# Strassen's algorithm inside the block products of the second feed-forward matmul, on one NeuronCore

## The chip, the cores and the metric

The kernel runs on one core of a Trainium2 chip. The metric is the device time of one execution in microseconds (us); less is better. Each time below is the median of several executions. "Before" is the kernel as it was and "after" the kernel with the change; PE is TensorE's matmul engine.

## The reference

The program is talking-heads attention, a Fourier mix, a normalization and a feed-forward network with a residual, all in float32. The change touches the second matrix product of the last line but one:

```python
u = x + np.real(fft2(x))                     # x: attention output, 8 x 448 rows of 768
un = (u - mean(u)) / sqrt(var(u) + 1e-6)
ch = np.maximum(un @ w_ch1, 0.0) @ w_ch2     # w_ch1: 768 x 3072, w_ch2: 3072 x 768
return u + ch
```

The 3584 rows are worked through in seven tiles of 512.

## The kernel before

Both feed-forward products already use Strassen's algorithm once, in the form with seven block products. For the second product the blocks of w2 (`w2f`) and their sums and differences (`w2s`) lie ready in DRAM; the sums were formed during the first tile. A tile of the second product is seven block products in the order `ORDER`, each of two halves of the contraction and two row blocks. The results that share a PSUM bank (keys P, Q and R) accumulate, and VectorE adds each of them into the residual `u`:

```python
def load_w2(i, half):
    w = pw2.tile([P, NQ, DH], F32, name="w2t", tag="w2t")      # 4 buffers
    of, n = {0: (w2f, 0), 1: (w2f, 2), ..., 6: (w2s, 0)}[i]    # cut
    nc.sync.dma_start(out=w[:, :, :], in_=of[n, half])
    return w

for n, i in enumerate(ORDER):                                  # 7 block products
    key = {0: "P", 5: "P", 6: "P", 3: "P", 1: "Q"}.get(i, "R")
    for half in range(2):
        w = load_w2(i, half)
        for x in range(NT2 // 2):                              # 2 row blocks
            ...
            for kf in range(NQ):                               # 6 steps
                nc.tensor.matmul(p, lhs[i][...], w[:, kf, :], ...)   # 384 columns
            if half == 0:
                continue
            for r, c in {...}[i]:                              # 1 or 2 quarters
                nc.vector.tensor_tensor(us_, us_, p, op=ALU.add)
    # after products 0 and 1: VectorE forms three differences of h each;
    # n = 1..4: normalization of the next tile
```

PE runs each float32 matmul of the code as two instructions. The framework, not the source, sets the order in which each engine gets its instructions. Each engine then works through its own queue in that order, as the traces show.

## Time and profile before

| | before |
|---|---|
| median, lowest and highest of 3 executions | 2750.27 us, 2742.7 to 2753.29 |
| attention and Fourier stage | to about 1113 us |
| preparation of the feed-forward | to 1155 us |
| second product, one tile | 111.0 us (the last 108.3) |
| second product, all seven tiles | 774.3 us |
| busy in the whole span: PE, VectorE (DVE), GpSimd (POOL) | 90%, 46%, 27% |
| mean granted clock of PE | 0.967 |

The lines that carry this are in the prediction. In short: in the second product PE is busy all the time and everything else has room, so this stage costs what the stream of matmuls costs.

### The profile page before, as it was taken

What the parts mean: (1) busy time and instruction counts of PE and PEld (TensorE: products, weight loads), DVE (VectorE), ACT (ScalarE), POOL (GpSimd) and SP (SyncE); (2) the same over time, 40 slices, a digit from 0 to 9 for tenths busy, and PEclk for the clock granted to TensorE, in tenths of its full rate; (3) what the DMA queues carried; (4) which work ended last, traced back from release to release, by engine and by line L of the source; (5) the groups of instructions that cost most, each with busy time, mean ns of one, the idle gap of its engine ahead of it and who ended that gap; (6) DMA issues with size and microseconds to landing.
All of it is one profiled execution on the core that took longest, in us unless ns stands there. A gap on an engine that the chain in (4) does not pass through costs nothing.

```text
span 2744.6 us, 46540 instructions
## 1 busy us (share of the span) xinstructions
PE 2476.4 (90%) x18544; PEld 1587.2 (58%) x18544; DVE 1262.2 (46%) x2238; ACT 724.0 (26%) x2135; POOL 732.0 (27%) x1117
## 2 busy tenths in 40 slices
PE   4778888888888886499999999999999999999998
PEld 2334344444444443387577678668658767866865
DVE  3887888888887876543032122213203212221220
ACT  2555555555555552110011001001001100100100
POOL 5465767666665544200100010010010000001000
PEclk7999999999999998799999999999999999999999
DMA  6665657575656457744444444444445444444432
GB/s 168 181 183 173 189 168 202 164 202 164 193 175 186 152 157 252 280 161 175 141 172 165 155 155 161 161 166 161 150 155 171 157 150 167 149 163 160 144 109 107
DMA packets 184471, 462.60 MB, mean 169 GB/s; under 512 B 23111, under 2 KB 129095, under 8 KB 171712
## 3 DMA queue, kind: packets, MB, share of 16 engines
q1 hardware_dynamic: 159968, 361.30, 38.7%
q0 software_dynamic: 24288, 98.33, 13.0%
q8 instruction: 148, 2.42, 0.4%
q14 instruction: 67, 0.55, 0.1%
HBM read 317.17 MB, written 59.79 MB: 137 GB/s over the span
## 4 chain that ended last, share of the span: by engine, by line
PE 41%; issue 9%; DMA 7%; DVE 1%; POOL 0%; SPq 0%; POOLq 0%; ACT 0%
PE psP L829 12%; PE psP L789 10%; PE psR L829 7%; PE psR L789 6%; PE psQ L829 3%; DMA w1t<-w1f 3%; PE psQ L789 2%; DMA u<-u_scr 2%; DMA out_dram<-u 2%; DMA w1t<-w1s 1%; PE psQ L759 1%; DVE st L746 0%; POOL ub L766 0%; DVE u L838 0%; SPq L703 0%
## 5 line engine op out<-in xcount | busy, mean ns | idle before, releaser
L789 PE MATMUL psP<-ub,w1t 128*128 128x256 f32 x2016 | 469.3, 386 | 26.6 <-DVE mv L748 16.9
L789 PEld LDWEIGHTS psP<-ub,w1t 128*128 128x128 f32 x2016 | 385.9, 193 | 94.7 <-DMA w1t<-w1f 22.1
L829 PE MATMUL psP<-w2t,h 128*128 128x384 f32 x1344 | 436.9, 486 | 0.0
L829 PEld LDWEIGHTS psP<-w2t,h 128*128 128x128 f32 x1344 | 254.4, 190 | 173.4
L323 ACT ACTIVATE PP<-mx,nmx 128x448 f32<-128x448 f32 x384 | 239.9, 629 | 376.2 <-DVE nmx L314 372.2
L766 POOL TENSOR_TENSOR ub<-ub 128x768 f32<-128x768 f32 x28 | 50.0, 1806 | 1036.2 <-ACT ub L761 1035.6
L336 POOL TENSOR_SCALAR PP<-PP,rcp 128x448 f32<-128x448 f32 x384 | 259.6, 686 | 154.0 <-DVE rcp L333 109.4
L307 PE MATMUL mx<-Kr,kw 60*64 60x448 f32 x1536 | 204.0, 589 | 97.0 <-ACT PP L323 88.2
L357 DVE STREAM_TRANSPOSE Pv<-po 128x896 f32<-128x896 f32 x192 | 212.9, 1109 | 101.4 <-PE po L346 101.2
L789 PE MATMUL psR<-ub,w1t 128*128 128x256 f32 x1008 | 232.1, 379 | 0.5 <-DMA w1t<-w1s 0.5
L314 DVE TENSOR_REDUCE nmx<-mx 128x2 f32<-128x896 f32 x192 | 206.2, 1074 | 34.9 <-PE mx L307 23.9
L829 PE MATMUL psR<-w2t,h 128*128 128x384 f32 x672 | 220.0, 486 | 0.0
L281 PE MATMUL ms<-kT,qT 64*64 64x448 f32 (+1 forms) x1536 | 205.3, 568 | 7.0 <-DVE X L475 6.3
L374 PEld LDWEIGHTS ms<-Pv,vv 64*64 64x64 f32 x5376 | 169.4, 142 | 67.2 <-issue 38.7
L128 ACT COPY Sb<-ms 124x448 f32<-124x448 f32 x379 | 186.5, 538 | 81.1 <-PE ms L281 66.1
L789 PEld LDWEIGHTS psR<-ub,w1t 128*128 128x128 f32 x1008 | 191.2, 190 | 27.8 <-DMA w1t<-w1s 1.9
L346 PE MATMUL po<-PP,kw 60*32 60x448 f32 x3072 | 194.1, 562 | 9.1 <-DVE rcp L333 7.7
L374 PE MATMUL ms<-Pv,vv 64*64 64x120 f32 x5376 | 181.0, 278 | 16.9 <-ACT Sb L128 15.4
L838 DVE TENSOR_TENSOR u<-u,psP 128x384 f32<-128x384 f32 x56 | 31.0, 554 | 341.6 <-PE psP L829 341.6
L829 PEld LDWEIGHTS psR<-w2t,h 128*128 128x128 f32 x672 | 126.3, 190 | 84.3
L307 PEld LDWEIGHTS mx<-Kr,kw 60*64 60x64 f32 x1536 | 42.2, 135 | 207.1 <-ACT PP L323 153.9
L761 ACT COPY ub<-psQ 128x384 f32<-128x384 f32 x56 | 25.0, 481 | 508.3 <-PE psQ L759 508.3
(92 smaller groups left out, 2604.4 us busy)
## 6 DMA issues: line engine op xcount, KB each, us to landing
Kr<-Sb SPq DMA_DIRECT2D x768, 105.0 KB
w2t<-w2s SPq DMA_DIRECT2D x56, 1152.0 KB
w2t<-w2f SPq DMA_DIRECT2D x42, 1152.0 KB
w1t<-w1s SPq DMA_DIRECT2D x72, 576.0 KB
raw<-in_moe_w_ch_dram POOLq DMA_DIRECT2D x96, 384.0 KB, 4.4
w1t<-w1f SPq DMA_DIRECT2D x84, 384.0 KB
w1t<-w1f SPq DMA_DIRECT2D x96, 192.0 KB
w1t<-w1s SPq DMA_DIRECT2D x72, 192.0 KB
```

What stands on the lines that cost most here:

```text
L128: self.nc.scalar.copy(out=out, in_=in_)
L281: nc.tensor.matmul(pss[x][64 * y:64 * y + r0 + 64 - lo, :S], st["qT", xx][64 * x:64 * x + 64, y, lo:r0 + 64], st["kT", xx][64 * x:64 * x + ...
L307: nc.tensor.matmul(mx[64 * z:64 * z + 64, x, :S], kw1[64 * x:64 * x + KR, :], Kr[64 * x:64 * x + KR, z, :], start=True, stop=True)
L314: nc.vector.tensor_reduce(nmx[:, :], steps[T]["mx"][:, :, :S], axis=AX.X, op=ALU.max, negate=True)
L323: nc.scalar.activation(PP[:, x, :], steps[T]["mx"][:, x, :S], ACTF.Exp, bias=steps[T]["nmx"][:, x:x + 1], accum_out=den[:, x:x + 1])
L336: nc.gpsimd.tensor_scalar(PP[:, x, :], PP[:, x, :], rcp[:, x:x + 1], 1.0, op0=ALU.mult, op1=ALU.mult)
L346: nc.tensor.matmul(po[o:o + 32, z, :S], kw2[64 * z:64 * z + KR, y, :], PP[64 * z:64 * z + KR, :, c * HS:(c + 1) * HS], start=True, stop=True)
L357: nc.vector.transpose(g["Pv"][:, T % GT, :].rearrange("p (z s) -> p z s", z=2), steps[T]["po"][:, :, :S])
L374: nc.tensor.matmul(pss[y][64 * x:64 * x + 64, :nu * R], st["v"][64 * y:64 * y + 64, i, jb * D:(jb + 1) * D], _ap(Pv, 64 * y * rp + 32 * jb ...
L766: nc.gpsimd.tensor_tensor(ub[:, o], ub[:, a], ub[:, b], op=ALU.subtract)
L789: nc.tensor.matmul(p, w[m][:, i, kc, :], ub[:, i, kc, :], start=opens and kc == 0, stop=kc == NK - 1, skip_group_check=True)
L829: nc.tensor.matmul(p, lhs[i][:, half * NQ + kf, x * P:(x + 1) * P], w[:, kf, :], start=opens and half == 0 and kf == 0, stop=half == 1 and ...
```

## The change

Strassen's algorithm is applied a second time, inside each of the seven block products. An outer product becomes seven inner products with half the rows, half the columns and half the contraction: 7 x 7 x 6 matmuls of 192 columns in place of 7 x 4 x 6 of 384, seven eighths of the columns. In exchange, every outer product needs four sums of w2's parts and four of h's parts, and more additions into `u`. The sums of w2 are formed while they are used, three on GpSimd and one on VectorE, one outer product ahead.

```diff
-    pw2 = pool("pw2", 4)
+    pw2 = pool("pw2", 9)
+    pss = pool("pss", 6)
     ...
+    def load_w2(i):
+        ... four parts b11, b12, b22, b21 are loaded
+        t1, t2, t4 = (w2_tile() for _ in range(3))
+        for o, x, y in ((t1, b12, b11), (t2, b22, t1), (b12, b22, b12), (t4, b21, t2)):
+            eng = nc.vector if o is b12 else nc.gpsimd
+            eng.tensor_tensor(o[:, :, :], x[:, :, :], y[:, :, :], op=ALU.subtract)
+        return b11, b21, b22, t4, t1, t2, b12
+
+    def sums_h(lhs):
+        ... s1, s2, s4, s3 = four tiles
+        for o, x, op, y in ((s1, a21, ALU.add, a22), (s2, s1, ALU.subtract, a11),
+                            (s4, a12, ALU.subtract, s2), (s3, a11, ALU.subtract, a21)):
+            nc.vector.tensor_tensor(o, x, y, op=op)
+        return a11, a12, s4, a22, s1, s2, s3
     ...
         for n, i in enumerate(ORDER):
-            ... two halves, two row blocks, 384 columns
+            bs, as_ = ready
+            for m, j in enumerate(INNER):             # INNER = 0, 1, 5, 4, 6, 2, 3
+                key = {0: "P", 5: "P", 6: "P", 3: "P", 1: "Q"}.get(j, "R")
+                ...
+                for kf in range(NQ):
+                    nc.tensor.matmul(p, as_[j][:, kf, :], bs[j][:, kf, :], ...)
+                for (r0, r1), (c0, c1) in PART[i]:    # result j into 1 to 4 parts of u
+                    nc.vector.tensor_tensor(us_, us_, ..., op=ALU.add)
+                if m == 1 and n + 1 < len(ORDER):
+                    ready = load_w2(ORDER[n + 1]), sums_h(lhs[ORDER[n + 1]])
```

The layouts of `w2f` and `w2s` in DRAM change to match (rows of 192 columns), and so does the code that forms w2's sums in the first tile; the pool of the normalized rows (`pun`) goes from two buffers to one. VectorE's sum, from here on "the own sum", is written over `b12`, which GpSimd's first sum reads. So the own sum must wait for GpSimd's first one.

More of the change, by code (lines that the diff above doesn't have):

```diff
@@ L634 @@
 ORDER = (0, 1, 4, 5, 2, 6, 3)
+INNER = (0, 1, 5, 4, 6, 2, 3)
+PART = {0: [((0, 2), (0, 2))], 1: [((0, 1), (0, 1))], 2: [((0, 1), (1, 2))],
+        3: [((1, 2), (0, 1))], 4: [((0, 2), (1, 2))],
+        5: [((0, 1), (1, 2)), ((1, 2), (0, 2))], 6: [((1, 2), (0, 2))]}
 NM = DFF // 2 // P
@@ L637 @@
 NQ = NM // 2
+DQ = DH // 2
 def _pieces(w_ch1, w_ch2, w1f, w2f):
@@ L655, in _pieces @@
             for j in range(2):
-                dst = w2f[2 * i + j, kf // NQ, :, kf % NQ, :]
+                dst = w2f[2 * i + j, kf // NQ, :, :, kf % NQ, :]
                 out.append((w_ch2, i * (DFF // 2) + kf * P, j * DH,
-                            dst.rearrange("p (m f) -> p m f", m=1), 1))
+                            dst.rearrange("m p f -> p m f"), 2))
     return out
@@ L671, in ffn_phase @@
     pw1 = pool("pw1", 3)
-    pw2 = pool("pw2", 4)
+    pw2 = pool("pw2", 9)
+    pss = pool("pss", 6)
     pu = pool("pu", 2)
-    pun = pool("pun", 2)
+    pun = pool("pun")
     pub = pool("pub")
@@ L714, in load_w1, with w2_tile @@
         return w
+    def w2_tile():
+        return pw2.tile([P, NQ, DQ], F32, name="w2t", tag="w2t")
     def sum_w2(kf):
-        w = pw2.tile([P, NQ, DH], F32, name="w2t", tag="w2t")
-        at = kf // NQ, slice(None), kf % NQ
-        nc.sync.dma_start(
-            out=w[:, 0:4, :],
-            in_=w2f[:, at[0], :, at[2], :].rearrange("b p d -> p b d"))
-        for o, a, b in ((4, 1, 0), (5, 3, 4), (1, 3, 1), (2, 2, 5)):
-            nc.vector.tensor_tensor(w[:, o], w[:, a], w[:, b], op=ALU.subtract)
@@ L724, in sum_w2 @@
-        for o, n in ((1, 0), (4, 2)):
-            nc.sync.dma_start(
-                out=w2s[n:n + 2, at[0], :, at[2], :].rearrange("b p d -> p b d"),
-                in_=w[:, o:o + 2, :])
-    def load_w2(i, half):
-        w = pw2.tile([P, NQ, DH], F32, name="w2t", tag="w2t")
+        at = kf // NQ, kf % NQ
+        ws = [w2_tile() for _ in range(4)]
+        b = []
+        for n in range(4):
+            t = ws[n // 2][:, 2 * (n % 2):2 * (n % 2) + 2, :]
+            nc.sync.dma_start(
+                out=t, in_=w2f[n, at[0], :, :, at[1], :].rearrange("c p d -> p c d"))
+            b.append(t)
@@ new lines, in sum_w2 @@
+        b11, b12, b21, b22 = b
+        t3, t1 = (ws[2 + n // 2][:, 2 * (n % 2):2 * (n % 2) + 2, :] for n in range(2))
+        t2, t4 = (ws[3][:, 2 * n:2 * n + 2, :] for n in range(2))
+        for o, x, y in ((t1, b12, b11), (t2, b22, t1), (t3, b22, b12), (t4, b21, t2)):
+            nc.vector.tensor_tensor(o, x, y, op=ALU.subtract)
+        for o, n in ((t3, 0), (t4, 1), (t1, 2), (t2, 3)):
+            nc.sync.dma_start(
+                out=w2s[n, at[0], :, :, at[1], :].rearrange("c p d -> p c d"), in_=o)
@@ L731, in load_w2 @@
+    def load_w2(i):
         of, n = {0: (w2f, 0), 1: (w2f, 2), 2: (w2f, 3), 3: (w2s, 1), 4: (w2s, 2),
                  5: (w2s, 3), 6: (w2s, 0)}[i]
-        nc.sync.dma_start(out=w[:, :, :], in_=of[n, half])
-        return w
+        w = {}
+        for r, c in ((0, 0), (0, 1), (1, 1), (1, 0)):
+            w[r, c] = w2_tile()
+            nc.sync.dma_start(out=w[r, c][:, :, :], in_=of[n, r, c])
+        b11, b12, b21, b22 = w[0, 0], w[0, 1], w[1, 0], w[1, 1]
+        t1, t2, t4 = (w2_tile() for _ in range(3))
[3 more added lines that the diff above has]
+        return b11, b21, b22, t4, t1, t2, b12
@@ new lines, in sums_h, with part @@
+    def sums_h(lhs):
+        def part(r, c):
+            return lhs[:, c * NQ:(c + 1) * NQ, r * P:(r + 1) * P]
+        a11, a12, a21, a22 = part(0, 0), part(0, 1), part(1, 0), part(1, 1)
+        s1, s2, s4, s3 = (pss.tile([P, NQ, P], F32, name="s", tag="s")[:, :, :]
+                          for _ in range(4))
+        for o, x, op, y in ((s1, a21, ALU.add, a22), (s2, s1, ALU.subtract, a11),
+                            (s4, a12, ALU.subtract, s2), (s3, a11, ALU.subtract, a21)):
+            nc.vector.tensor_tensor(o, x, y, op=op)
+        return a11, a12, s4, a22, s1, s2, s3
@@ L817, in second @@
         u = us.pop(t)
-        ps = {}
+        ru = _row(u)
+        ready = load_w2(ORDER[0]), sums_h(lhs[ORDER[0]])
         for n, i in enumerate(ORDER):
-            key = {0: "P", 5: "P", 6: "P", 3: "P", 1: "Q"}.get(i, "R")
-            opens = i in (0, 1, 4)
-            for half in range(2):
-                w = load_w2(i, half)
-                for x in range(NT2 // 2):
-                    if opens and half == 0:
-                        ps[key, x] = ps_tile(key)
-                    p = ps[key, x][:, :DH]
-                    for kf in range(NQ):
-                        nc.tensor.matmul(
-                            p, lhs[i][:, half * NQ + kf, x * P:(x + 1) * P], w[:, kf, :],
-                            start=opens and half == 0 and kf == 0,
-                            stop=half == 1 and kf == NQ - 1, skip_group_check=True)
-                    if half == 0:
-                        continue
-                    for r, c in {0: [(0, 0)], 1: [(0, 0)], 4: [(1, 1)], 5: [(0, 1)],
-                                 2: [(0, 1)], 6: [(1, 1)], 3: [(1, 0)]}[i]:
-                        us_ = u[:, 2 * r + x, c * DH:(c + 1) * DH]
-                        nc.vector.tensor_tensor(us_, us_, p, op=ALU.add)
@@ new lines, in second @@
+            bs, as_ = ready
+            ps = {}
+            for m, j in enumerate(INNER):
+                key = {0: "P", 5: "P", 6: "P", 3: "P", 1: "Q"}.get(j, "R")
+                if j in (0, 1, 4):
+                    ps[key] = ps_tile(key)
+                p = ps[key][:, :DQ]
+                for kf in range(NQ):
+                    nc.tensor.matmul(p, as_[j][:, kf, :], bs[j][:, kf, :],
+                                     start=j in (0, 1, 4) and kf == 0,
+                                     stop=kf == NQ - 1, skip_group_check=True)
+                r2, c2 = {0: (0, 0), 1: (0, 0), 4: (1, 1), 5: (0, 1), 2: (0, 1),
+                          6: (1, 1), 3: (1, 0)}[j]
+                for (r0, r1), (c0, c1) in PART[i]:
+                    dims = [[ru, P], [2 * DM, r1 - r0], [DH, c1 - c0], [1, DQ]]
+                    us_ = _ap(u, (2 * r0 + r2) * DM + c0 * DH + c2 * DQ, dims)
+                    nc.vector.tensor_tensor(
+                        us_, us_, _ap(ps[key], 0, [[_row(ps[key]), P], [0, r1 - r0],
+                                                   [0, c1 - c0], [1, DQ]]), op=ALU.add)
+                if m == 1 and n + 1 < len(ORDER):
+                    ready = load_w2(ORDER[n + 1]), sums_h(lhs[ORDER[n + 1]])
@@ L883 @@
     w1f = scr.tile([NM, P, 4, NK, P], F32, name="w1f")
-    w2f = scr.tile([4, 2, P, NQ, DH], F32, name="w2f")
+    w2f = scr.tile([4, 2, 2, P, NQ, DH // 2], F32, name="w2f")
     w1s = scr.tile([NM, P, 4, NK, P], F32, name="w1s")
-    w2s = scr.tile([4, 2, P, NQ, DH], F32, name="w2s")
+    w2s = scr.tile([4, 2, 2, P, NQ, DH // 2], F32, name="w2s")
     mix_phase(tc, ident, q, k, v, w_pre, w_post, u_scr,
```

## The prediction

> **What bounds the kernel now.** I read the page first: its busy table, its slices, its chain of waits and its groups; then the stretches by stage, then the timeline of single stretches. The kernel has three parts: an attention and Fourier stage to about 1113 us, a preparation to 1155 us, and seven tiles of the feed-forward from there to 2745 us.
>
> ```profile
> PE 2476.4 (90%) x18544; PEld 1587.2 (58%) x18544; DVE 1262.2 (46%) x2238; ACT 724.0 (26%) x2135; POOL 732.0 (27%) x1117
> ...
> PE   4778888888888886499999999999999999999998
> ...
> DVE  3887888888887876543032122213203212221220
> ...
> POOL 5465767666665544200100010010010000001000
> PEclk7999999999999998799999999999999999999999
> ```
>
> From slice 17 on, PE is at 9 with nothing near it: VectorE is at 0 to 3 tenths, GpSimd at 0 to 1, the clock is full. The second product (line 829) is part of that. Two tiles by stage, first product, then second (start:end, length, busy time of each engine with its instruction count):
>
> ```profile
> 1387.00:1505.00 118.00, 113.88 (x499) 95.03 (x498) 36.54 (x82) 16.50 (x44) 3.15 (x5) 0.99 0.48 160
> 1505.00:1616.00 111.00, 111.00 (x379) 69.52 (x378) 16.23 (x24) 5.77 (x14) 8.68 (x6) 1.00 0.43 157
> ```
>
> In the second product PE is busy 111.00 of 111.00 us, VectorE 16 us, GpSimd 9 us. So that stage is the matmul stream itself, and anything that shortens the stream shortens the kernel, as long as the other engines still fit beside it.
>
> How long is one instruction of that stream? The duration of a matmul includes its latency, so I take the spacing from the timeline:
>
> ```profile
> 1509.18 15.64 PE L829 MATMUL psQ<-w2t,h 128*128 128x384 f32 x48
> ...
> 1524.66 0.49 PE L759 MATMUL psQ<-ident,un 128*128 128x128 f32 x3
> ```
>
> The groups give 486 ns for one of line 829, so 48 of them in 15.64 us are spaced (15.64 - 0.486) / 47 = 322.4 ns. Line 789 has 256 columns, and the chain of waits shows 12 of them as pieces of 2.59 us, or 215.8 ns. The slope is (322.4 - 215.8) / 128 = 0.833 ns a column, with 2.5 ns fixed. A float32 product is two such instructions (1344 + 672 + 336 = 2352 at line 829 for the 1176 calls that the code makes).
>
> **What the Trainium skill says.** "TensorE: Matmul & The Clock Gate", section "LDWEIGHTS (loading the stationary operand)", makes a weight load columns / 1.2 ns, 107 ns for 128 columns. The trace shows 190 ns for each, which would exceed the new matmuls; but that includes a tail. Four loads of 113 columns, each about 178 ns long by the trace, occupy 0.49 us together, and their matmuls were 107 ns apart:
>
> ```profile
> 1089.58 0.49 PEld L416 LDWEIGHTS ms<-ident,XT 128*113 128x113 f32 x4 [0.35 <-ACT XT L396]
> ```
>
> So a load occupies the path for about 107 ns, and 192 columns (162 ns) hide it. "SBUF — State Buffer", section "Who interferes with whom", says that VectorE instructions with two SBUF inputs and GpSimd instructions that read SBUF exclude each other for a whole instruction. The trace agrees:
>
> ```profile
> 275.71 1.91 POOL L432 TENSOR_TENSOR xd<-X 112x768 f32<-112x768 f32 x1
> ...
> 275.98 2.05 DVE L521 SCALAR_TENSOR_TENSOR tmp<-raw,tmp 128x384 f32<-128x384 uint32 x1
> ```
>
> The VectorE instruction takes 0.514 us at its shortest. Here it began inside the GpSimd one (275.71 to 277.62) and ended at 278.03, 0.41 us after it. This lock is what my prediction turns on. "GPSIMD Engine Reference", section "Engine selection", advises against two-input elementwise work there, about 2 times slower; this trace has 1.80 us for 768 elements, where VectorE's line would give 0.96.
>
> **The change, part by part, for one tile.**
> *Matmuls.* Before: 336 instructions x 322.4 = 108.3 us. After: 7 x 7 x 6 products of 192 columns, two instructions each, 588 x (192 x 0.833 + 2.5 = 162.4) = 95.5 us. Gain 12.8 us, over 7 tiles 90 us (3.3%). The 24 transposes at 109 ns (2.6 us) stay.
> *VectorE rates.* 512 to 1024 elements cost 0.692 to 1.225 us, so 1.041 ns an element and 0.16 fixed; adds from PSUM fit the same line (384 in 0.554).
> *Adds into u.* Before 14 x 0.554 = 7.8 us. The outer level no longer accumulates in PSUM, so each of 49 results is added to all its quarters: outer products need 4, 1, 1, 1, 2, 1+2 and 2 blocks of 192. One is 0.96 us, four are 0.36, three are 0.56; sum 4.1 us, times 7 inner results 28.5 us. These have one input in PSUM and are free of the lock.
> *Sums of h.* 28 of 768 elements at 0.96 us = 26.8 us, under the lock.
> *Sums of w2.* Three of four on GpSimd, 1152 elements. GpSimd's 383 and 768 elements take 0.985 and 1.80 us, so 1152 take an estimated 2.62 us; 21 x 2.62 = 55 us under the lock. One on VectorE: 7 x 1.36 = 9.5 us, under the lock.
> *Already there.* Six subtractions of h at 1.225 us (7.4 us, lock), GpSimd's four of ub at 1.80 us (7.2 us, lock), norm 8 us on VectorE.
> *DMA.* The seven loads move the same bytes in 4608-byte rows in place of 9216; the share of 0.43 leaves room. In the first tile, w2's sums have 768-byte rows in place of 1536, and four buffers of nine each in place of one of four: two pieces in flight, not four. I put 10 us on that, a guess from the DMA-bound stretch of 1064 to 1153 us.
>
> Sums: VectorE 28.5 + 26.8 + 9.5 + 7.4 + 8 = 80 us and GpSimd 62 us, beside 98 us of PE. Each fits alone. The lock carries 55 + 7.2 + 26.8 + 9.5 + 7.4 = 106 us. Perhaps 4 to 12 us of it (the first product's sums) fall under the first product's matmuls. So 94 to 102 us stand beside 98 us: the lock is as full as PE.
>
> **What a full lock does.** An inner product lasts L = 12 x 0.162 = 1.95 us, an outer one 13.6 us (before: 48 x 0.3224 = 15.5 us). In the order 0, 1, 5, 4, 6, 2, 3, results 0, 5, 6, 3 share one PSUM bank and 4, 2 another, so each add must be done within one L of its result. VectorE works in order; an add queued behind a sum that is locked out by a 2.62 us GpSimd instruction misses this. Walking a middle product: at 5.8 us result 5 is ready, one s goes (0.96), then its add; GpSimd's first sum takes 6.8 to 9.4. The next s, due at 7.8, waits to 9.4 and runs to 10.4; the add of result 4 follows at about 10.9, and PE, which needs it at 9.7, loses 1.1 us. GpSimd's second sum has the lock to 13.0. If VectorE's own w2 sum is queued ahead of the add of result 6, it ends at 14.4, that add at 14.7, and PE loses another 2 us; if behind, nothing. So 14.6 or 16.7 us for 15.5 before. The outer products with h's subtractions or ub's four fare worse; the last of a tile, with no s to make, better. I take 15.7 us as the mean: 7 x 7 x 0.2 = +10 us, and +10 us for the preparation: 2770 us.
>
> **Rivals.**
> *The lock hides.* If orders fall well, the whole matmul gain stays: 2750 - 90 = 2660 us. For it: VectorE and GpSimd alone fit, and the inner order and buffer counts look tuned. Against it: 94 to 102 us of lock time in 98 with hard deadlines. Half of the gain would be 2705.
> *Head of line.* Waits placed by an order that expects faster transfers or a faster GpSimd already occur: in five of the seven tiles VectorE waits some 3.5 us for u's load with adds behind it, and PE with it (about 3.2 us near 1620). If the VectorE w2 sum, which waits for loads and for GpSimd's first sum, is queued before the adds of results 4 or 6 in every product, 3 to 5 us go each time; 49 x 3 less the 90 gives 2810, with 5 us 2900.
> *Weight loads.* If a load really held the path for 190 ns, 588 x 190 = 112 us, +3.4 us a tile: 2774 with no other cost. The 113-column loads speak against it.
> *DMA.* Weights wanted at 16.5 MB per 98 us, with fewer spare buffers. The share of 0.43 makes this the least likely.
>
> **Range and chances.** Only a nearly hidden lock gives faster by over 2% (below 2695): 0.22. Partial stalls that eat the gain: 0.43. Head-of-line waits on top (above 2805): 0.35. The range, 2690 to 2875, has half of the gain and more at one end and 4 us of stall an outer product at the other.
>
> **What would show it.** Right: 192-column matmuls 162 ns apart; GpSimd sums of 2.6 us; VectorE SBUF sums (0.96 alone) with a mean well above that and maxima of 3 us or more; PE waiting at the inner products of line 829's successor for VectorE's adds into u, 1 to 3 us an outer product; second-product stages of 105 to 120 us with PE below 95% busy. Wrong: these stages at 98 to 101 us with PE full (the lock hides); matmul spacing near 190 ns (weight loads); PE waiting for w2 transfers; or a longer stretch before 1155 us that exceeds 15 us.

## The result

| | before | after |
|---|---|---|
| median (lowest to highest), 4 executions each | 2746.48 us (2742.55 to 2753.29) | 2954.14 us (2949.35 to 2960.16) |
| ratio of after to before, 95% interval | | 1.0754 (1.0722 to 1.0787) |
| start of the first tile's second product | 1266.8 us | 1270.8 us |
| second product, sum of seven tiles | 774.3 us | 984.4 us |
| mean granted clock of PE | 0.967 | 0.931 |

A ratio here is the mean time of one kernel's executions over that of the other's of the same rounds, so it is not quite the ratio of the medians that stand beside it.

The kernel became 7.5% slower. The second product's tiles alone lengthened by 984.4 - 774.3 = 210.1 us; by the medians, everything else together changed by some 2 us.

The page of the changed kernel; the lines are busy times over the span, then tenths of busy time in 40 slices, with the granted clock last:

```profile
PE 2493.0 (84%) x20308; PEld 1894.5 (64%) x20308; DVE 1807.7 (61%) x2777; ACT 725.2 (25%) x2135; POOL 1226.4 (42%) x1264
...
PE   4878888888888875987998898799789879979987
...
DVE  3878887888888755575356427535642753563374
...
POOL 4575665667665432145114504511540451153043
PEclk8999999999999987998998999899899999989988
```

Where PE stood at 9 before, in every slice from 17 to 38 (counted from 0), it now swings between 7 and 9, and in most of the slices with a 7 the clock falls to 8. The slices with a 7 are ones in which GpSimd has 3 to 5 tenths, where it had 0 or 1 before, and VectorE 4 to 6, where it had 0 to 4: the second products.

One second product of the changed kernel by stretch (start:end, length, busy time of each engine with its instruction count, granted clock, DMA share, GB/s). The tile before took 111.00 us with PE busy 111.00:

```profile
1528.50:1671.20 142.70, 114.56 (x614) 111.67 (x614) 90.12 (x95) 4.02 (x9) 76.75 (x25) 0.88 0.39 129
```

PE is busy 114.56 us of 142.70, although the new stream was to need 98. Nothing has become full in its place: VectorE is busy 90 us, GpSimd 77, the DMA share is 0.39. So a wait became the bound, and the clock is at 0.88.

The groups name the wait (count, busy us and mean ns of one, then the idle time before these instructions and what ended it):

```profile
L759 POOL TENSOR_TENSOR w2t<-w2t 128x1152 f32<-128x1152 f32 x147 | 493.1, 3354 | 1077.6 <-issue 483.6
...
L867 PE MATMUL psR<-w2t,s 128*128 128x192 f32 x1176 | 275.0, 396 | 155.7 <-DVE u L875 155.7
...
L771 DVE TENSOR_TENSOR s<-h 128x768 f32<-128x768 f32 x98 | 257.3, 2626 | 4.9 <-ACT h L843 4.7
...
L867 PE MATMUL psP<-w2t,s 128*128 128x192 f32 x1176 | 221.7, 341 | 39.3 <-DVE u L875 39.3
```

PE was idle 155.7 + 39.3 = 195.0 us before these matmuls, and VectorE's additions into `u` ended all of it. GpSimd's sums take 3354 ns in the mean, and half of VectorE's sums of h (98 of 196), which take 0.95 us alone, 2626 ns.

One of these stalls in the timeline (start, length, engine, what; in brackets the idle time before and what ended it). PE first:

```profile
1557.27 2.22 PE L867 MATMUL psP<-w2t,s 128*128 128x192 f32 x12
...
1564.42 4.21 PE L867 MATMUL psR<-w2t,s 128*128 128x192 f32 x12 [4.49 <-DVE u L875]
1568.42 2.98 PE L867 MATMUL psP<-w2t,h 128*128 128x192 f32 x12
```

The matmuls of inner result 2 (the psR line at 1564.42) could not start before VectorE had emptied the bank of result 4. PE stood still for 4.49 us, and the next twelve instructions took 4.21 us where twelve normally take 2.1. VectorE in the same stretch:

```profile
1555.99 0.96 DVE L771 TENSOR_TENSOR s<-h,s 128x768 f32<-128x768 f32 x1 [1.71 <-PE psP L867]
1556.87 0.35 DVE L875 TENSOR_TENSOR u<-u,psP 128x192 f32<-128x192 f32 x1
1559.46 1.36 DVE L759 TENSOR_TENSOR w2t<-w2t 128x1152 f32<-128x1152 f32 x1 [2.24 <-POOL w2t L759]
1560.73 3.37 DVE L771 TENSOR_TENSOR s<-h 128x768 f32<-128x768 f32 x1
1564.02 0.34 DVE L875 TENSOR_TENSOR u<-u,psR 128x192 f32<-128x192 f32 x1
```

At 1559.46 VectorE runs the own sum, after 2.24 us of doing nothing: it waited for GpSimd's first sum. That one in turn had started late, at the end of an inner product:

```profile
1556.09 10.48 POOL L759 TENSOR_TENSOR w2t<-w2t 128x1152 f32<-128x1152 f32 x3 [10.92 <-PE psP L867]
```

By the code it needs from PE only a buffer of w2's parts that is given back there. Behind the own sum in VectorE's queue comes a sum of h that is held by the lock (3.37 us for work of 0.95). Only then comes the addition of result 4, at 1564.02, although this result had lain ready since about 1557.3. The chain of waits says the same in order of time (start, length, what):

```profile
1556.09 3.34 POOL w2t L759
...
1559.46 1.36 DVE w2t L759
1560.82 3.28 DVE s L771
1564.10 0.28 DVE u L875
...
1564.42 4.21 PE psR L867 x12
```

GpSimd's first sum, VectorE's own sum, the locked-out sum of h, the addition, and then PE: no gap between them.

In the records of single instructions this happens 42 times, in the first six of the seven outer products of all seven tiles (the seventh prepares no sums), with 3.6 to 4.8 us of idle time each, 185.4 us in all. After a stall, 8 to 17 matmuls, 12 in the mean, start at about twice the normal distance, mostly 320 ns where 162.5 is normal. Counting the distances of 240 to 450 ns, there are some 555 wide ones in the seven second products.

### The profile page after: what moved, and what is told of

Read it like the earlier page. It is cut to its first block, busy times and chain, and to the rows that moved or that the text cites. A ratio compares the mean times of both kernels' runs of the same rounds, so it can differ in the third digit from the quotient of the medians. Undisturbed runs are those within 1.5% of the kernel's fastest.

```text
span 2952.0 us, 51502 instructions
## 1 busy us (share of the span) xinstructions
PE 2493.0 (84%) x20308; PEld 1894.5 (64%) x20308; DVE 1807.7 (61%) x2777; ACT 725.2 (25%) x2135; POOL 1226.4 (42%) x1264
## 4 chain that ended last, share of the span: by engine, by line
PE 37%; issue 20%; DVE 16%; POOL 10%; DMA 9%; ACT 3%; SPq 1%; POOLq 0%; ACTq 0%; DVEq 0%
PE psP L867 9%; PE psR L867 6%; POOL w2t L759 6%; DVE s L771 5%; PE psP L827 4%; PE mx L307 3%; PE ms L374 3%; PE psQ L867 3%; DVE nmx L314 3%; PE po L346 3%; ACT PP L323 2%; DVE w2t L759 2%; PE ms L281 2%; PE ms L462 2%; PE psR L827 2%
## 5 line engine op out<-in xcount | busy, mean ns | idle before, releaser
L759 POOL TENSOR_TENSOR w2t<-w2t 128x1152 f32<-128x1152 f32 x147 | 493.1, 3354 | 1077.6 <-issue 483.6
L867 PE MATMUL psR<-w2t,s 128*128 128x192 f32 x1176 | 275.0, 396 | 155.7 <-DVE u L875 155.7
L867 PEld LDWEIGHTS psR<-w2t,s 128*128 128x128 f32 x1176 | 249.5, 237 | 167.1 <-DVE u L875 167.1
L771 DVE TENSOR_TENSOR s<-h 128x768 f32<-128x768 f32 x98 | 257.3, 2626 | 4.9 <-ACT h L843 4.7
L867 PE MATMUL psP<-w2t,s 128*128 128x192 f32 x1176 | 221.7, 341 | 39.3 <-DVE u L875 39.3
L867 PEld LDWEIGHTS psP<-w2t,s 128*128 128x128 f32 x1176 | 202.5, 198 | 46.4 <-DVE u L875 46.1
L867 PE MATMUL psP<-w2t,h 128*128 128x192 f32 x1176 | 219.7, 339 | 0.1
L867 PEld LDWEIGHTS psP<-w2t,h 128*128 128x128 f32 x1176 | 208.3, 203 | 2.7 <-issue 1.9
L374 PE MATMUL ms<-Pv,vv 64*64 64x120 f32 x5376 | 181.0, 282 | 15.7 <-ACT Sb L128 15.4
```

The costliest lines, as they stand in the source:

```text
L374: nc.tensor.matmul(pss[y][64 * x:64 * x + 64, :nu * R], st["v"][64 * y:64 * y + 64, i, jb * D:(jb + 1) * D], _ap(Pv, 64 * y * rp + 32 * jb ...
L759: eng.tensor_tensor(o[:, :, :], x[:, :, :], y[:, :, :], op=ALU.subtract)
L771: nc.vector.tensor_tensor(o, x, y, op=op)
L867: nc.tensor.matmul(p, as_[j][:, kf, :], bs[j][:, kf, :], start=j in (0, 1, 4) and kf == 0, stop=kf == NQ - 1, skip_group_check=True)
```

## The experiments

Two theories were put against each other. The first: **place in the queue**. The own sum waits in VectorE's queue for GpSimd and holds up finished results, and the stall then drops the clock. The rival: **the lock and the work**. VectorE and GpSimd simply have too much to read through what they share, and the time would stay long wherever the sums stand. The runs came in three groups, each with its own executions of before (medians 2751.34, 2747.09 and 2751.74 us). All kernels but the two that are called wrong gave correct results.

| run | median, us | ratio to before (95%) | second product, middle tiles, us |
|---|---|---|---|
| e1 no sums of w2 (wrong) | 2662.49 | 0.9672 (0.9643 to 0.9702) | 100.0 |
| e7 without the own sum only (wrong) | 2713.62 | 0.9872 (0.9855 to 0.9889) | 107.7 |
| e10 own sum moved behind additions | 2751.4 | 1.0000 (0.9968 to 1.0032) | 112.6 to 114.3 |
| e2 all sums on VectorE | 2724.13 | 0.9902 (0.9865 to 0.9939) | 111.1 to 113.7 |
| e3 all sums on GpSimd | 2782.4 | 1.0126 (1.0094 to 1.0158) | 115.8 to 117.8 |
| e4 own sum in its own tile | 2867.51 | 1.0430 (1.0402 to 1.0458) | 125 to 131 |
| e6 filler matmuls | 2930.41 | 1.0660 (1.0629 to 1.0691) | 139 to 140 |
| e8 sums stored, seven parts loaded | 2671.73 | 0.9728 (0.9710 to 0.9745) | 100.0 |
| e9 two sums stored, two formed | 2673.26 | 0.9729 (0.9710 to 0.9747) | 100.0 to 101.3 |
| after | 2954.14 | 1.0754 (1.0722 to 1.0787) | 140.2 to 142.8 |

### e1: no sums of w2 at all

Wrong on purpose: parts that have no sum stand in their place, so the matmuls, the additions and h's sums stay.

```diff
-        t1, t2, t4 = (w2_tile() for _ in range(3))
-        for o, x, y in (...): eng.tensor_tensor(o, x, y, op=ALU.subtract)
-        return b11, b21, b22, t4, t1, t2, b12
+        return b11, b21, b22, b21, b12, b22, b12
```

> Wrong result on purpose: the four weight sums of each product are left out and the loaded quarters are used in their place; matmuls, loads, sums of h and adds stay. My theory (VectorE's own weight sum waits for GpSimd ahead of the add that PE needs, and the clock drops in the stall): with no sum there is neither wait nor lock, so the 42 stalls of 4.7 us and the slow matmuls behind them go, the second product takes 98 to 102 us a tile and the kernel 2660 to 2690 us. Rival (VectorE has too much work of its own, adds and sums of h): stages of 110 us or more and 2750 us or more.

Measured: 2662.49 us, with a relative error of 0.92. Six tiles take 100.0 us and the last 96.0, sum 696. VectorE is busy 58 us in such a tile, 6.6 us of PE's idle time and 27 wide distances are left in all. So the shorter stream, the additions and the sums of h are all but hidden, and the gain in the matmuls is real: (1 - 0.9672) x 2750 = 90 us. The whole loss comes from the sums of w2, with the waits and the buffers that they bring.

### e2: all four sums on VectorE

```diff
-            eng = nc.vector if o is b12 else nc.gpsimd
+            eng = nc.vector
```

> All four weight sums on VectorE, GpSimd idle. No lock and no wait on GpSimd, but VectorE gets 21 x 1.36 = 28 us more a tile, about 108 us in all beside 98 us of PE. My theory: no stalls of 4 us, yet VectorE bound, stages of 108 to 120 us, 2740 to 2830 us. Rival (the lock's total time is what costs, not the place in the queue): the same kernel without the lock would be at 2700 us or less.

Measured: 2724.13 us, below what I expected, though not as low as the rival had it. The tiles take 111 to 114 us, and VectorE is busy 95 us of them. Against my expectation stalls are left: 13 waits of PE, 52.1 us together and up to 5.5 us long, all for VectorE's additions, which here stand behind VectorE's own sums. One of them, VectorE first, then PE:

```profile
1574.66 2.95 DVE L759 TENSOR_TENSOR w2t<-w2t 128x1152 f32<-128x1152 f32 x1
1577.54 0.34 DVE L875 TENSOR_TENSOR u<-u,psP 128x192 f32<-128x192 f32 x1
```

```profile
1577.93 2.29 PE L867 MATMUL psP<-w2t,s 128*128 128x192 f32 x6 [4.92 <-DVE u L875]
```

There is more work on VectorE than after has, and no lock against GpSimd's sums; yet the kernel is 230 us faster than after. It is not VectorE's amount of work that makes after slow. It doesn't rule the lock out.

### e3: all four sums on GpSimd

```diff
-            eng = nc.vector if o is b12 else nc.gpsimd
+            eng = nc.gpsimd
```

> All four weight sums on GpSimd, so nothing in VectorE's queue waits for GpSimd's result, but the time under the shared lock grows from 106 to about 115 us a tile. My theory: the stall shrinks from 4.7 us to 0 to 1.5 us per product, too short for the clock to drop, and the kernel takes 2690 to 2770 us. Rival (the total of the lock): at or above the changed kernel's 2954 us, some 9 us a tile more, 3000 us.

Measured: 2782.4 us, some 12 us above the range of my theory and 172 us below after. GpSimd reads more than in after, so the lock is asked for more; if the lock were what costs, this should have been slower than after. GpSimd's timeline shows what is left:

```profile
1581.36 13.25 POOL L759 TENSOR_TENSOR w2t<-w2t 128x1152 f32<-128x1152 f32 x4 [3.15 <-PE psP L867]
```

Four sums take 13.25 us, and an outer product's matmuls alone take 84 x 0.1625 = 13.65. Yet over a tile of 117.7 us GpSimd is busy 91.8, so it is not full. PE stands still for 13.2 us of that tile, nearly all of it before VectorE's additions; by the trace these stand behind sums of h that the lock stretches (2061 and 2283 ns in the mean, where 0.95 us is normal). Seven stalls of some 3.7 us are left in the seven second products.

### e6: filler matmuls against the drop of the clock

24 matmul instructions with an unused result stand between the fifth and the sixth inner product, where PE stood still:

```diff
+                if j == 6 and n + 1 < len(ORDER):
+                    dummy = ps_tile("Q")[:, :DQ]
+                    for kf in range(2 * NQ):
+                        nc.tensor.matmul(dummy, as_[2][:, kf % NQ, :], bs[2][:, kf % NQ, :],
+                                         start=kf == 0, stop=kf == 2 * NQ - 1, ...)
```

> The changed kernel with 24 matmul instructions (3.9 us) into an unread PSUM bank between the fifth and the sixth inner product of the first six outer ones, where PE waits 4.7 us anyway. My theory of the clock: PE no longer idles long enough for the clock to drop, the 11 matmuls at double spacing after each stall go, 42 x 1.85 = 78 us less: 2865 to 2900 us. Rival (they are slow for another reason, such as their operands): 2950 us or more.

Measured: 2930.41 us, 30 us above the 2900 that I expected at most. PE's timeline shows a filler and what follows it:

```profile
1564.83 4.06 PE L873 MATMUL psQ<-w2t,s 128*128 128x192 f32 x24
1569.79 2.22 PE L867 MATMUL psR<-w2t,s 128*128 128x192 f32 x12 [0.89 <-DVE u L881]
```

With the filler, the wait before the psR line is 0.89 us, and its twelve instructions take 2.22 us, not 4.21. The number of wide distances fell from 555 to 137. So it is the standing still that brings the wide distances, and filling it keeps the clock, whose mean is 0.969 here and 0.931 in after: 418 x 0.1575 = 66 us less. But 42 fillers of 3.9 us cost 164 us, while PE's idle time before the second product's matmuls fell by only 107 (195.0 to 87.6 us): new waits of about 1.2 us came behind the fillers, and one stall of 4.4 us per tile stayed. These three terms sum to -9 us; the measured ratios give (1.0660 - 1.0754) x 2750 = -26. Of the 17 between, 11 lie ahead of the first filler: the first second product of this profile started at 1259.8 us, that of after at 1270.8. The rest is not accounted for. So the run shows the cause of the wide distances and their number, and not their price to the microsecond.

### e4: the own sum in a tile of its own

If the own sum isn't written over `b12`, it need not wait for GpSimd. It takes a tenth buffer.

```diff
-        t1, t2, t4 = (w2_tile() for _ in range(3))
+        t1, t3, t2, t4 = (w2_tile() for _ in range(4))
-        for o, x, y in ((t1, b12, b11), (t2, b22, t1), (b12, b22, b12), (t4, b21, t2)):
-            eng = nc.vector if o is b12 else nc.gpsimd
+        for o, x, y in ((t1, b12, b11), (t3, b22, b12), (t2, b22, t1), (t4, b21, t2)):
+            eng = nc.vector if o is t3 else nc.gpsimd
-    pw2 = pool("pw2", 9)
+    pw2 = pool("pw2", 10)
```

> VectorE's weight sum writes a tile of its own (ten buffers, not nine) in place of the one that GpSimd's first sum reads: the same four sums on the same engines, the same time under the lock, but the wait for GpSimd's result is gone. My theory (that wait at the head of VectorE's queue makes the stall 4.7 us and so drops the clock): the stall falls to some 2.5 us, which is the lock alone, the clock stays, 2760 to 2850 us. Rival (the lock alone makes the stall, the wait only hides inside it): 2900 us or more.

Measured: 2867.51 us, above my range by 17 us. It regains less than half of the loss: 42 stalls are left, of 142.9 us together. VectorE's timeline, then PE's:

```profile
1578.44 1.36 DVE L759 TENSOR_TENSOR w2t<-w2t 128x1152 f32<-128x1152 f32 x1 [3.61 <-PE psQ L797]
1579.72 0.95 DVE L771 TENSOR_TENSOR s<-h,s 128x768 f32<-128x768 f32 x1
1580.59 3.37 DVE L771 TENSOR_TENSOR s<-h 128x768 f32<-128x768 f32 x1
1583.87 0.81 DVE L875 TENSOR_TENSOR u<-u,psP 128x192 f32<-128x192 f32 x2
```

```profile
1584.73 3.74 PE L867 MATMUL psP<-w2t,s 128*128 128x192 f32 x12 [4.90 <-DVE u L875]
```

VectorE still stands 3.61 us before the own sum. The chain of waits shows for what: a buffer that PE gave back at 1571.4 and a transfer of a part of w2 into it, until 1578.15. The trace's mark "PE psQ" is only the last event that it saw. One wait took the place of the other, and the own sum with two sums of h stands in front of two finished results again. The bad place in the queue is what stayed the same.

### e7: only the own sum left out

Wrong on purpose: GpSimd's three sums stay, `b12` is used as it is.

```diff
-        for o, x, y in ((t1, b12, b11), (t2, b22, t1), (b12, b22, b12), (t4, b21, t2)):
+        for o, x, y in ((t1, b12, b11), (t2, b22, t1), (t4, b21, t2)):
+            nc.gpsimd.tensor_tensor(o, x, y, op=ALU.subtract)
```

> Wrong result on purpose: only VectorE's own weight sum is left out, GpSimd keeps its three. Neither the wait nor the 1.36 us are there; the lock between GpSimd's sums and VectorE's sums of h stays, 96 us a tile. My theory: what is left above the 2662 us without any sum is the lock's own price, 2720 to 2775 us, and so the wait with its clock drop is the larger part, 180 to 230 us. Rival (the lock is the larger part): 2850 us or more.

Measured: 2713.62 us, with a relative error of 0.90; 6 us below my range. No wait of PE over 1.4 us is left; all of them come to 47 us and end with VectorE's additions. With GpSimd's three sums and VectorE's sums of h against each other, this is the price of GpSimd's sums without the own sum: (0.9872 - 0.9672) x 2750 = 55 us over e1. By the waits most of it is the lock; no run separates it from the three buffers more that each product holds here than in e1.

### e10: the own sum moved behind the additions

Nothing is taken away. The own sum is put into VectorE's queue behind the addition of the sixth inner result; the framework offers an edge for the order.

```diff
-        ... (b12, b22, b12) on nc.vector within load_w2
+        late.append(lambda: nc.vector.tensor_tensor(b12, b22, b12, op=ALU.subtract))
     ...
+                if m == 5 and n + 1 < len(ORDER):
+                    with tc.issue_after(add.ins):
+                        late.pop()()
```

> The changed kernel with one thing moved: VectorE's own weight sum is queued behind the add of the sixth inner product, not ahead of the add of the fourth. Same instructions, same engines, same buffers, same time under the lock, and the sum still reads what GpSimd's first sum has read. My theory (its place in the queue makes the long stall): stalls of 1 us or so as without that sum, no slow matmuls, 2714 us plus a little for its 1.36 us under the lock, 2715 to 2770 us. Rival (the sum's work and lock time, not its place): 2900 us or more.

Measured: 2751.4 us, in the range. VectorE's timeline, then PE's:

```profile
1573.84 2.31 DVE L774 TENSOR_TENSOR s<-h 128x768 f32<-128x768 f32 x1 [0.73 <-PE psR L871]
1576.07 0.34 DVE L879 TENSOR_TENSOR u<-u,psR 128x192 f32<-128x192 f32 x1
...
1576.79 2.66 DVE L774 TENSOR_TENSOR s<-h 128x768 f32<-128x768 f32 x1
1579.37 0.34 DVE L879 TENSOR_TENSOR u<-u,psR 128x192 f32<-128x192 f32 x1
1579.63 3.52 DVE L761 TENSOR_TENSOR w2t<-w2t 128x1152 f32<-128x1152 f32 x1
```

```profile
1573.64 2.11 PE L871 MATMUL psP<-w2t,s 128*128 128x192 f32 x12
1576.47 2.22 PE L871 MATMUL psR<-w2t,s 128*128 128x192 f32 x12 [0.71 <-DVE u L879]
```

The additions (L879) now come between the sums of h, and the own sum comes after them, in 3.52 us because the lock holds it. PE loses 0.71 us here, and 1.31 us at 1586.51, where an addition stands behind the own sum and one more sum of h; no wait is of the old length. In the second products no wait of PE above 2.0 us is left, and 118 wide distances of 555 remain. With the same work on the same engines, the place of one instruction of 1.36 us makes (1.0754 - 1.0000) x 2750 = 207 us. (The framework moved one neighbour with it: the addition of the fifth result, at 1576.52, now runs ahead of a sum of h, not behind it.) The rival theory, that the lock and the work cost this whatever the order, falls with this run.

### e8 and e9: the sums formed once

If forming the sums at each use costs time in any place, they can be stored in the first tile and loaded afterwards. The matrix w2 is the same for all seven tiles. In e8 the later tiles load seven parts; in e9 they load five and VectorE forms two.

```diff
+    w2x = scr.tile([7, 4, P, NQ, DH // 2], F32, name="w2x")      # in DRAM
     ...
+        if t:      # e8: later tiles load b11, b21, t2, t1, t3, b22, t4
+        else:      # first tile: sums on nc.vector, then stored to w2x[i, 0..3]
     ...
+        if t:      # e9: load b11, b21, t2, t1, b22, then on VectorE:
+            for o, x, y in ((t3, t2, b11), (t4, b21, t2)):
+                nc.vector.tensor_tensor(o, x, y, op=ALU.subtract)
```

> The first tile makes the four sums on VectorE and stores them; the other six tiles load all seven parts and sum nothing. VectorE 61 us a stage, GpSimd free, no lock; but the second product loads 28.9 MB in 100 us, 290 GB/s, where the busiest stretch of the traces so far moved 331. My theory: the stages of six tiles take 100 to 104 us as without sums, the first 112 to 120, the kernel 2675 to 2710 us. Rival (the transfers become the bound): stages of 110 us and more with PE waiting for w2 transfers, 2740 us or more.

> As the stored sums, but two sums are stored and five parts loaded (20.6 MB, 206 GB/s); the other two sums are made on VectorE straight from loaded parts (t3 = t2 - b11), so none waits for another sum. VectorE about 80 us a stage, no lock. Theory: stages of 100 to 104 us in six tiles, 2680 to 2715 us. Rival (VectorE's queue is already too slow at 80 of 100 us): stages of 107 us or more, 2730 us or more.

Measured: 2671.73 us for e8 and 2673.26 us for e9; each lies a little below the range that I gave it (2675 and 2680 us at the low end). A later tile of e8:

```profile
1500.50:1600.50 100.00, 98.91 (x603) 97.21 (x602) 53.37 (x86) 4.57 (x11) 7.95 (x5) 1.00 0.89 306
```

PE is busy 98.91 us of 100.00 at the full clock. The transfers pay for it, with a share of 0.89 and 306 GB/s, where after has 0.39. The first tile, which forms the sums, takes 110.7 us. e9 moves less and has VectorE at 75 us of 100, and its time is the same as e8's within the intervals. Both beat the kernel before by 2.7%, and by the ratios they lie (0.9728 - 0.9672) x 2750 = 15 us above e1, which has no sums to form or to load.

## Why the prediction was wrong

The prediction said 2770 us, 2690 to 2875, and 2954.14 lies outside.

**The stream and the weight loads: right.** It had 162.4 ns for 192 columns and a gain of 90 us. In the changed kernel and in e10 twelve instructions start 1.95 us after the twelve before, which is 162.5 ns each, and e1 shows the gain of 90 us when nothing waits. The rival of the weight loads (190 ns) is out.

**Work of VectorE and GpSimd: right, and of no use.** One, two or four quarters of an addition cost 0.35, 0.55 and 0.95 us, as worked out. GpSimd's sum was estimated at 2.62 us; the shortest was 2.617. Neither engine became full.

**The preparation: not settled.** +10 us was a guess. The first second product started 1270.8 - 1266.8 = 4 us later; but the first product before it began 6.8 us earlier than in the profile of before and so lasted 10.8 us longer, and one profile of each doesn't tell which of the two the change made.

**Two readings, off without effect.** The line 1505:1616 lies 11 us late: that second product ran from 1493.7 to 1604.7, with PE busy 111.00 of 111.00 as well. And in slice 17 VectorE is at 4 tenths, not at 0 to 3.

**The lock: right as a cost, somewhat larger than walked.** The walk lost 1.1 us an outer product if the own sum stood behind the additions. In e10 PE is idle for 73.6 us over 49 outer products, 1.5 each, and in e7 for 47.3, 1.0 each; the tiles take 113 and 107.7. An outer product of e10 is 113 / 7 = 16.1 us, where the walk gave 14.6 with the own sum in the good place. What it missed is that GpSimd's sums are themselves held up, to 3.35 us in the mean.

**The step that failed** is the place of the own sum. The walk put it behind the addition of result 4: "If VectorE's own w2 sum is queued ahead of the add of result 6, it ends at 14.4, that add at 14.7, and PE loses another 2 us; if behind, nothing. So 14.6 or 16.7 us". From this came the mean of 15.7. The trace has it two places earlier: ahead of one sum of h and of the addition of result 4. There it waits 2.24 us for GpSimd, and the sum of h behind it runs into GpSimd's second sum, so the addition comes at 1564.02 instead of about 1557.3. PE loses 4.4 us in the mean (185.4 / 42), in 42 of the 49 outer products. An outer product with a stall lasts 21.0 us in the mean, not 15.7.

This is the **head-of-line rival**, which the prediction wrote down and priced ("3 to 5 us go each time", with 5 us 2900) but took as the less likely way. Its size of the stall was right, though it counted 49 stalls where 42 came. Its total was not, since it lacked a term: **the clock**. The Trainium skill, "TensorE: Matmul & The Clock Gate", section "HAM oscillation — how this bites in real kernels", warns of "PE-idle gaps >~3.4µs", after which the matmuls run at half speed for a while. The trace agrees: after 3.6 to 4.8 us of idle time the distance doubles to 320 ns, for 12 instructions in the mean, and the fillers of e6 bring the wide distances from 555 to 137. I had read this page for the loads alone. The sum, from e1's tiles:

| term | us |
|---|---|
| e1's second products, no sums of w2 | 696 |
| PE idle for VectorE's additions (155.7 + 39.3, less e1's 6.6) | 188 |
| wide distances, (555 - 27) x 0.1575 | 83 |
| sum | 967 |
| measured | 984.4 |

So over e1, the stalls are 188 us and the clock 83, and 17 us are in neither term. An estimate of those: some 8 us, because a matmul's record (326 ns) ends 0.16 us after the next could have started, at each of 48 waits more; and the first distance after a stall, 0.45 to 0.5 us in 31 cases, which was not counted as wide. The stalls alone would have made 2750 - 90 + 188 = 2848 us, inside the range; the clock took it out.

By the runs, in ratios times 2750: no sums of w2 2660; with GpSimd's three sums and the lock +55; with the own sum in a place that harms little +35; with it ahead of finished results another 207, which is idle time and clock together.

**What stays open:** why the framework placed the own sum there. That it expected GpSimd's sum to end sooner than it does would explain it, but no run tests this. Nor does a run test the other cure: GpSimd's first sum waits for PE 40 times, 393.7 us in all, by the code for a buffer. With more buffers it might have started early enough for the own sum to do no harm in its old place; the tenth buffer of e4 went to the new tile.

## What to carry to other kernels

On an engine that works in order, ask for each new instruction what it waits for and who stands behind it, before you ask how long it takes: here one instruction of 1.36 us, moved behind a few additions, was worth 7.5% of the kernel. A stall of PE of some 4 us costs nearly half as much again in clock, so many such stalls should be priced at about 1.5 times their length (288 / 188 here, the whole difference to e1 over its stalls). And a sum that is formed anew at each use, of operands that don't change, can be stored and loaded while the transfers have room, as e8 did.

## What the Trainium skill lacked or had wrong

- "TensorE: Matmul & The Clock Gate", on the length of a gap that slows the clock (about 3.4 us): the direction holds, yet the limit isn't sharp here. In the second products of all the runs, no wait of PE of 0.2 to 1.9 us (294 of them) is followed by more than one wide distance. Of six waits of 1.97 us in e10, four are followed by 11; of 35 waits of 2.5 to 3.5 us, 17 by 8 to 18 and the others by one; of 78 longer ones, 76 by 8 to 18.
  It makes weight loads 107 ns for 128 columns, while the trace records 190 ns each; matmuls 162.5 ns apart with such a load for each show that at least 28 ns of the record don't hold up the stream.
- "SBUF — State Buffer" is right about the lock, but doesn't say what becomes of a row of GpSimd sums against VectorE's: a sum of 2.62 us took 3.35 in the mean and a VectorE sum of 0.95 us up to 3.37.
- No page that I looked up says what an instruction costs that waits at the head of an in-order queue ahead of results that are ready: 207 us here, against 55 us for GpSimd's three sums with the lock.
